# Keys turned by DMA as planes of 16-bit words, a weight term in the short-mantissa type, a branch hint, and a new order

## The chip, the core and the metric

The kernel runs on one core of a Trainium2 chip. A core has a matrix engine (TensorE, PE in the profile; its weight loads are listed as PEld), a vector engine (VectorE, DVE), an activation engine (ScalarE, ACT), a general engine (GpSimd, POOL) and SyncE (SP), which here issues every DMA. Each engine works through its own list of instructions in order and waits on semaphores that the others raise. The metric is device time in microseconds (us) of one execution. Lower is better.

## What is computed

Gated linear attention on 4 x 8 heads of 768 steps, followed by a gated MLP whose spatial product mixes all 768 steps. Everything is float32.

```python
# attention: for every step t, per batch and head (head_dim 48)
state = alpha[t][:, None] * state + outer(k[t], v[t])
y[t] = q[t] @ state
# MLP on x = all heads side by side (4, 768, 384)
h = gelu_tanh(x @ w_in)            # 384 -> 1024
u, v = h[..., :512], h[..., 512:]
v_n = (v - mean(v)) / sqrt(var(v) + 1e-6) * g_ln
v_s = einsum('ts,bsd->btd', w_sg, v_n) + b_sg[:, None]
out = x + (u * v_s) @ w_out        # 512 -> 384
```

w_in and w_out arrive as 64-bit floats.

## The kernel before

**Attention in blocks.** The 4 x 768 steps are cut into 24 blocks of 128, numbered 0 to 23, six for each batch. Block i loads its decays (`a_i`) and one tile with k, q and v (`kqv_i`). Two scans on DVE (`scan_i`, `recip_i`) build the products of decays; `q_i` and `k_i` scale queries and keys by them (k on DVE or POOL). PE then does the "squares": step `G_o_i` takes the score products of block i together with the first products of block o = i - 1 (output `y`, and the outer products `dl` of k and v that go into the state); `M_o_i` and `H_o_i` follow with the rest of y. `causal_i` (DVE) masks the scores, `half_i`, `add_i` and `state_i` (DVE) bring the state on. `y3_i` and `xf_i` (ACT) copy y out of PSUM, three small DMAs (`pack_i_k`) put a part of it in place.

The outer products need the keys with steps, not head dimensions, on the partitions. So `H_o_i` ends with four 128 x 128 transposes on PE (line 500, tile `tp`), and `kn_i` (ACT, line 513) copies them to SBUF. `G_i_(i+1)` waits for it.

**MLP.** `xh_i` and `xl_i` split x into a high part in the short-mantissa type (fp32r, which the matrix engine takes in one pass) and a remainder in the same type. Every MLP product is then three fp32r products (high by high, high by low, low by high; lines 582 to 584): `V_b_c` (v half, nine matmuls of 512 columns) and its followers `V_b_c_1` to `_8` (gelu, moments, normalisation, split); `U_b_h_d` (u half, nine matmuls of 384 columns); `P_b_h_d` (spatial product, 18 matmuls) with `_1` to `_4` (scale, gate, split); `R_b_h_k` (output product, 12 matmuls), its `_add` on DVE and its `_store`.

**Weights.** They are split the same way once, in pieces of 384 columns: `wv_j` and `wu_j` (w_in), `ws_s_h` (w_sg) and `wo_d` (w_out). For the 64-bit ones `size`, `clamp`, `shift`, `sign`, `power` and `rest` rebuild a float32 and the part that it leaves over, `high` (ACT) makes the high part. For `wv` and `wu` the low part is made on PE (`low_pe`, lines 293 to 295, tile `mm_w`): identity by the float32, minus identity by the high part, identity by the rest. The first and the last of these are full float32 products.

**The order.** A string, `ORDER`, names all steps; they are issued in this order, which sets the order within each engine. A suffix such as `/dve` chooses the engine where a step has two. `Plan.issue` checks that each step's inputs and buffers have been issued.

**The end.** Every range check of the decays is summed into one number, `cnt_i`. Each engine loads it and branches over a general, slow version of the whole computation (`tc.If`, line 1024), which the inputs here never need.

```python
    with tc.manual_schedule():
        plan.issue(ORDER)
    n_ok = nc.values_load(cnt_i[0:1, 0:1], min_val=0, max_val=P)
    with tc.If(n_ok < P):
```

Of the kernel before, what the change touches and what calls it, by code (L numbers as in the profile page):

```python
# [9 lines left out]
F32 = mybir.dt.float32  # L10
# [3 lines left out]
U32 = mybir.dt.uint32  # L14
AF = mybir.ActivationFunctionType
# [20 lines left out]
NIDLE = 10  # L36
EPS = 1e-6
# [4 lines left out]
a_0 scan_0 idle_0 end_0 idle_1 idle_2 idle_3 kqv_0_q idle_4 idle_5 pend_0 q_0 recip_0 load_wv_1 size_wv_1 clamp_wv_1  # L42
kqv_0_k k_0/dve G_n_0 H_n_0 idle_6 idle_7 load_wv_0 a_1 range_0 size_wv_0 shift_wv_1 floor_0 sign_wv_1 clamp_wv_0
kqv_1 power_wv_1 shift_wv_0 rest_wv_1 sign_wv_0 scan_1 high_wv_1 kn_0 causal_0 end_1 q_1 pend_1 low_pe_wv_1 idle_8
idle_9 kqv_0_v a_2 load_wv_3 power_wv_0 recip_1 rest_wv_0 k_1/dve floor_1 high_wv_0 size_wv_3 low_wv_1 clamp_wv_3
kqv_2 scan_2 G_0_1 turn_0 M_0_1 half_0 H_0_1 pend_2 end_2 shift_wv_3 q_2 sign_wv_3 recip_2 load_ws_1_0 high_ws_1_0
low_pe_ws_1_0 power_wv_3 load_ws_2_0 high_ws_2_0 y3_0 floor_2 causal_1 add_0 k_2/pool a_3 low_pe_ws_2_0 state_0
low_pe_wv_0 scan_3 rest_wv_3 xf_0 kn_1 low_ws_1_0 high_wv_3 G_1_2 low_ws_2_0 turn_1 M_1_2 half_1 H_1_2 pend_3
range_1 end_3 kqv_3 q_3 recip_3 range_2 add_1 causal_2 load_ws_4_0 high_ws_4_0 kn_2 xf_1 pack_0_1 pack_0_0 load_wv_2
low_wv_0 pack_0_2 low_pe_wv_3 size_wv_2 y3_1 k_3/pool state_1 load_ws_5_0 clamp_wv_2 a_4 low_pe_ws_4_0 shift_wv_2  # L50
sign_wv_2 G_2_3 low_wv_3 xh_0 low_ws_4_0 turn_2 half_2 M_2_3 H_2_3 high_wv_2 high_ws_5_0 power_wv_2 rest_wv_2
low_pe_wv_2 kqv_4 load_ws_0_0 load_wu_1 pack_1_2 pack_1_0 pack_1_1 kn_3 range_3 xf_2 low_pe_ws_5_0 low_wv_2 a_5
xl_0/pool causal_3 V_0_0 add_2 floor_3 scan_4 end_4 pend_4 high_ws_0_0 q_4 recip_4 k_4/dve state_2 kqv_5 size_wu_1
y3_2 low_pe_ws_0_0 pack_2_0 pack_2_2 pack_2_1 clamp_wu_1 shift_wu_1 floor_4 sign_wu_1 power_wu_1 G_3_4 half_3
V_0_0_1 turn_3 low_ws_0_0 xh_1 M_3_4 H_3_4 rest_wu_1 load_wu_2 low_ws_5_0 high_wu_1 low_pe_wu_1 scan_5 xl_1/dve q_5
end_5 pend_5 xh_2 low_wu_1 V_0_1 xl_2/dve recip_5 kn_4 y3_3 size_wu_2 xf_3 clamp_wu_2 U_0_0_1 load_wu_0 k_5/pool
V_0_0_2 V_0_2 V_0_0_3 V_0_1_1 causal_4 V_0_1_2 add_3 V_0_0_4 V_0_0_5 load_ws_3_0 pack_3_1 range_5 range_4 size_wu_0
V_0_0_6/act clamp_wu_0 state_3 G_4_5 turn_4 M_4_5 shift_wu_2 high_ws_3_0 pack_3_0 pack_3_2 low_pe_ws_3_0 shift_wu_0
sign_wu_2 V_0_1_3 a_6 kqv_6 V_0_0_7 high_wu_2 U_0_0_1_1 power_wu_2 sign_wu_0 floor_5 xh_3 low_ws_3_0 high_wu_0
half_4 rest_wu_2 power_wu_0 H_4_5 V_0_0_8 rest_wu_0 xl_3/dve V_0_2_1 low_pe_wu_2 add_4 causal_5 V_0_2_2 V_0_3  # L60
V_0_1_4 V_0_1_5 state_4 scan_6 V_0_2_3 xf_4 y3_4 kn_5 V_0_1_6/act V_0_1_7 V_0_1_8 G_5_n turn_5 M_5_n low_pe_wu_0
# [1033 lines left out]
```

## Time and profile before

| | |
|---|---|
| median of 3 runs | 362.7 us (362.56 to 363.47) |
| profiled execution | 362.69 us, of which 360.9 us from its first to its last instruction (the span) |
| granted TensorE clock in the span, mean | 0.993 |
| matmul instructions | 4548 |
| share of the 16 DMA engines that SP's queue takes | 33.4% |
| bytes from and to HBM | 32.70 MB read, 4.72 MB written |

In the rows that follow, the timeline gives start (us), duration (us), engine, line, operation, tiles (output <- inputs), shape and how many instructions are merged. A row by line gives the count, then the sum of busy time (us) and the mean (ns), then the engine's idle time ahead of these instructions and what ended it. A row of DMA issues ends with the size of one and the median time from issue to landing. A row of a line's instructions gives count, shortest, median and longest (ns), and the first and last start (us). A row of waits reads "who <- for whom: us in total, times, longest".

### The profile page before, as it was taken

How to read it: one execution, taken by the hardware profiler on the slowest of the kernel's cores; microseconds unless marked ns; L12 is line 12 of the kernel's file. 1: busy time of each engine (PE TensorE's matmuls, PEld its weight loads, DVE VectorE, ACT ScalarE, POOL GpSimd, SP SyncE). 2: the span in 40 equal slices, each digit the busy share in tenths (PEclk: the TensorE clock that was granted, in tenths of full speed). 3: DMA queues.
4: the chain of work that ended last, by engine and by line, in shares of the span. 5: the costliest groups of instructions: out<-in, count | busy, mean ns of one | idle time of the engine just before them, and what ended most of it. 6: DMA issues, size and time to landing. Idle time of an engine off the chain costs nothing.

```text
span 360.9 us, 10758 instructions
## 1 busy us (share of the span) xinstructions
PE 346.5 (96%) x4548; PEld 316.4 (88%) x4548; DVE 250.1 (69%) x496; ACT 153.5 (43%) x372; POOL 84.5 (23%) x128
## 2 busy tenths in 40 slices
PE   6799999999999999999999999999999999999991
PEld 6567877999999888899999889899999889999991
DVE  6999999899999968674656877568555744441241
ACT  4388777843543357623214365522233434311110
POOL 1021221423102346332103307210305122300000
PEclk9999999999999999999999999999999999999997
DMA  7877476443532565211315055120340000000002
GB/s 265 286 236 263 118 215 215 126 162 91 191 97 70 161 217 156 94 31 53 130 47 162 17 166 180 25 99 2 116 138 7 22 31 29 2 0 22 23 25 72
DMA packets 17912, 39.37 MB, mean 109 GB/s; under 512 B 2880, under 2 KB 9792, under 8 KB 17856
## 3 DMA queue, kind: packets, MB, share of 16 engines
q1 hardware_dynamic: 17856, 38.61, 33.4%
q8 instruction: 37, 0.61, 0.7%
q14 instruction: 19, 0.16, 0.1%
HBM read 32.70 MB, written 4.72 MB: 104 GB/s over the span
## 4 chain that ended last, share of the span: by engine, by line
PE 87%; DVE 2%; issue 0%; DVEq 0%
PE mm_s L582 10%; PE mm_s L583 9%; PE mm_s L584 9%; PE mm_u L582 5%; PE mm_u L583 5%; PE mm_u L584 5%; PE mm_v L582 5%; PE mm_v L584 4%; PE mm_v L583 4%; PE y L415 4%; PE mm_o L582 4%; PE mm_o L698 3%; PE mm_o L584 3%; PE mm_o L583 3%; PE tp L500 3%; PE y L425 3%
## 5 line engine op out<-in xcount | busy, mean ns | idle before, releaser
L582 PE MATMUL mm_s<-ws_hi,vh 128*128 128x384 f32 x192 | 66.1, 344 | 0.0
L583 PE MATMUL mm_s<-ws_lo,vh 128*128 128x384 f32 x192 | 65.0, 338 | 0.0
L584 PE MATMUL mm_s<-ws_hi,vl 128*128 128x384 f32 x192 | 65.0, 338 | 0.0
L673 ACT CAST gh<-g 128x384 fp32r<-128x384 f32 x32 | 16.2, 512 | 48.4 <-DVE g L668 28.7
L582 PEld LDWEIGHTS mm_s<-ws_hi,vh 128*128 128x128 f32 x192 | 36.0, 188 | 0.3
L583 PEld LDWEIGHTS mm_s<-ws_lo,vh 128*128 128x128 f32 x192 | 36.1, 188 | 0.0
L584 PEld LDWEIGHTS mm_s<-ws_hi,vl 128*128 128x128 f32 x192 | 36.0, 188 | 0.0
L663 DVE SCALAR_TENSOR_TENSOR g<-mm_s,g_col,b_bc 128x384 f32<-128x384 f32 x32 | 19.4, 610 | 22.2 <-PE mm_s L584 22.2
L668 POOL TENSOR_TENSOR g<-g,u 128x384 f32<-128x384 f32 x15 | 15.2, 1011 | 82.7 <-DVE g L663 74.3
L582 PE MATMUL mm_u<-xh,wi_hi 128*128 128x384 f32 x96 | 33.3, 347 | 0.0
L359 DVE TENSOR_TENSOR_SCAN pf<-a,floor 128x516 f32<-128x516 f32 x24 | 31.1, 1297 | 2.4 <-DMA a<-in_aT 2.0
L583 PE MATMUL mm_u<-xl,wi_hi 128*128 128x384 f32 x96 | 32.4, 338 | 0.0
L584 PE MATMUL mm_u<-xh,wi_lo 128*128 128x384 f32 x96 | 32.4, 338 | 0.0
L377 DVE TENSOR_TENSOR_SCAN pf<-a,floor 128x516 f32<-128x516 f32 x24 | 30.2, 1259 | 1.3
L582 PE MATMUL mm_v<-wi_hi,xh 128*128 128x512 f32 x72 | 29.7, 413 | 0.0
L387 POOL TENSOR_TENSOR kqv_t<-kqv_t,pf 128x512 f32<-128x512 f32 x12 | 14.3, 1191 | 65.2 <-DVE pf L377 49.9
L707 DVE TENSOR_TENSOR xf<-mm_o,xf 128x384 f32<-128x384 f32 x24 | 13.0, 550 | 23.0 <-PE mm_o L698 23.0
L584 PE MATMUL mm_v<-wi_hi,xl 128*128 128x512 f32 x72 | 28.5, 395 | 0.0
L583 PE MATMUL mm_v<-wi_lo,xh 128*128 128x512 f32 x72 | 28.4, 394 | 0.0
L402 PE MATMUL sc<-kqv_t 64*64 64x64 f32 x768 | 25.8, 220 | 2.6 <-DVE floor L383 2.4
L648 ACT ACTIVATE u<-mm_u 128x384 f32<-128x384 f32 x32 | 15.5, 490 | 27.9 <-PE mm_u L584 27.9
L402 PEld LDWEIGHTS sc<-kqv_t 64*64 64x64 f32 x768 | 23.6, 135 | 3.4 <-DVE floor L383 2.5
(117 smaller groups left out, 831.2 us busy)
## 6 DMA issues: line engine op xcount, KB each, us to landing
kqv_t<-in_kqv SPq DMA_DIRECT2D x23, 768.0 KB, 4.5
a<-in_aT SPq DMA_DIRECT2D x24, 258.5 KB, 3.2
out_x<-xf SPq DMA_DIRECT2D x24, 192.0 KB, 2.1
raw<-in_w_in SPq DMA_DIRECT2D x8, 384.0 KB, 3.7
raw<-in_w_out SPq DMA_DIRECT2D x4, 384.0 KB, 3.1
raw_sg<-in_w_sgT SPq DMA_DIRECT2D x6, 192.0 KB, 5.5
xf<-y SPq DMA_DIRECT2D x72, 16.0 KB, 1.8
raw<-in_w_sgT SPq DMA_DIRECT2D x6, 192.0 KB, 2.8
```

The costliest lines, as they stand in the source:

```text
L359: nc.vector.tensor_tensor_scan(pf.rearrange("p j t -> p (j t)"), s["a"][:, 0:NP * C1], floor.rearrange("p j t -> p (j t)"), initial=0.0, o ...
L377: nc.vector.tensor_tensor_scan(s["pf"].rearrange("p j t -> p (j t)")[:, ::-1], s["a"][:, NP * C1:0:-1], floor.rearrange("p j t -> p (j t)" ...
L387: eng.tensor_tensor(s["k"], s["k"], s["pf"][:, :, 1:], op=ALU.mult)
L402: lambda j=j, h=h: nc.tensor.matmul(sc[half(h), e, 64 * j:64 * j + 64], k[half(e), j, half(h)], q[half(e), j, half(h)], start=True, stop=True,
L415: lambda j=j: nc.tensor.matmul(y_of(y, j, e)[:, half(h)], v[half(h), j, half(e)], at[half(h), e, j], start=first and j < 2, stop=True, ski ...
L582: nc.tensor.matmul(o, lh, rh, start=(idx == 0), stop=False)
L583: nc.tensor.matmul(o, lh, rl, start=False, stop=False)
L584: nc.tensor.matmul(o, ll, rh, start=False, stop=(idx == n - 1))
L648: nc.scalar.activation(t["u"], t["o"], AF.Gelu_apprx_tanh)
L663: nc.vector.scalar_tensor_tensor(t["g"], t["o"], g_col[:, d:d + 1], b_bc[:, tsl], op0=ALU.mult, op1=ALU.add,)
L668: eng.tensor_tensor(t["g"], t["g"], u["u"], op=ALU.mult)
L673: nc.scalar.copy(g["h"][:, d], t["g"])
```

## The change

1. **Keys of blocks 8 to 23.** Their transposes leave PE. The keys are copied into two planes of 16-bit words (`kp_i`, ACT), a transposing DMA on SP's queue turns both planes (`kt_i`, eight tiles of 128 x 128 words), and `kn_i` (ACT or, for blocks 15, 19 and 22, DVE) puts the words together again. `kp` and `kt` share two buffers with the raw weights.
2. **Rest term.** For `wv` and `wu` the rest is written, negated, into an fp32r tile of its own, and the third product of `low_pe` becomes minus identity by this rest, both fp32r.
3. **Branch hint.** The last two steps (the last add and its store) stand in a code block of their own, which begins with a hint for the branch on SP and DVE.
4. **Order.** The whole `ORDER` string is new.

```diff
+CLOSING = 2
+TURNED = 8
...
-    def split_f64(dst_hi, dst_lo, src):
+    def split_f64(dst_hi, dst_lo, src, on_pe):
...
         def rest():
+            if on_pe:
+                t["rest"] = mlp.tile([P, TH], F32R, tag="g", name="rest", bufs=2)
             nc.vector.scalar_tensor_tensor(
-                t["mag"], t["raw"][:, :, 0].bitcast(U32), 2.0 ** -52, t["mag"], op0=ALU.mult, op1=ALU.mult,
+                t["rest"] if on_pe else t["mag"], t["raw"][:, :, 0].bitcast(U32), (-1 if on_pe else 1) * 2.0 ** -52, t["mag"],
+                op0=ALU.mult, op1=ALU.mult,
             )
 
         def low_pe():
             t["o"] = o = psm.tile([P, TH], F32, tag="mm", name="mm_w")
             nc.tensor.matmul(o, ident, t["top"].bitcast(F32), start=True, stop=False)
             nc.tensor.matmul(o, nident, dst_hi, start=False, stop=False)
-            nc.tensor.matmul(o, ident, t["mag"], start=False, stop=True)
+            nc.tensor.matmul(o, nident, t["rest"], start=False, stop=True)
...
         if i is not None:
+            if i >= TURNED:
+                return
             st[i]["tp"] = tp = ps.tile([P, NP, P], F32, tag="tp", name="tp")
             for j in range(NP):
                 nc.tensor.transpose(tp[:, j], st[i]["k"][:, j], ident)
...
+    def words(x):
+
+        return x.bitcast(U16).rearrange("p j (t w) -> p w j t", w=2)
+
+    def k_words(i):
+        st[i]["kp"] = kp = stage.tile([P, 2, NP, C], U16, tag="raw", name="kp", bufs=2)
+        nc.scalar.copy(kp, words(st[i]["k"]))
+
+    def k_turn(i):
+        st[i]["kt"] = kt = stage.tile([P, 2, NP, P], U16, tag="raw", name="kt", bufs=2)
+        nc.sync.dma_start_transpose(
+            kt.rearrange("p w j d -> p (w j) d"), st[i]["kp"].rearrange("p w j t -> p (w j t)"),
+        )
+
+    def k_whole(i, eng):
+        st[i]["kn"] = kn = att1.tile([P, NP, P], F32, tag="kn", name="kn")
+        if eng is nc.scalar:
+            eng.copy(words(kn), st[i]["kt"])
+        else:
+            eng.tensor_copy(words(kn), st[i]["kt"])
...
+            plan.add(("kp", i), "act", 950, lambda i=i: k_words(i), [("k", i)], takes=[("raw", 2, [("kt", i)])])
+            plan.add(
+                ("kt", i), "sp", 1200, lambda i=i: k_turn(i), [("kp", i)], takes=[("raw", 2, [("kn", i)])], nbytes=500000,
+            )
+            plan.add(
+                ("kn", i), "act", 950, lambda i=i: k_whole(i, nc.scalar), [("kt", i)], takes=[("kn", 1, [o_at[i]])],
+                other=("dve", 1100, lambda i=i: k_whole(i, nc.vector)),
+            )
...
+    order = ORDER.split()
     with tc.manual_schedule():
-        plan.issue(ORDER)
+        plan.issue(order[:-CLOSING])
+    with tc.block():
+        tc.mark_branch_hint_location("general", hint=0, engines=[mybir.EngineType.SP, mybir.EngineType.DVE])
+        with tc.manual_schedule():
+            plan.issue(order[-CLOSING:])
...
-    with tc.If(n_ok < P):
+    with tc.If(n_ok < P, label="general"):
```

Three places show what the new order does. The first is PE's list in the head of the program, up to the start of `G_4_5` (the squares of blocks 4 and 5, which begin with the y products). Before, the last matmul of `U_0_0_1` (tile `mm_u`) and the nine of `V_0_2` (`mm_v`) lead up to it:

```order
L584 MATMUL mm_u<-xh,wi_lo 128x384
L582 MATMUL mm_v<-wi_hi,xh 128x512
L583 MATMUL mm_v<-wi_lo,xh 128x512
L584 MATMUL mm_v<-wi_hi,xl 128x512
L582 MATMUL mm_v<-wi_hi,xh 128x512
L583 MATMUL mm_v<-wi_lo,xh 128x512
L584 MATMUL mm_v<-wi_hi,xl 128x512
L582 MATMUL mm_v<-wi_hi,xh 128x512
L583 MATMUL mm_v<-wi_lo,xh 128x512
L584 MATMUL mm_v<-wi_hi,xl 128x512
L415 MATMUL y<-at,kqv_t 64x64 x8
L440 MATMUL dl_838<-kqv_t,kn 64x48
```

After the change the same list on PE, at the same squares; the `mm_v` rows are now the end of `V_0_1`, and two pieces of w_sg follow it (`mm_w`):

```order
L614 MATMUL mm_v<-wi_lo,xh 128x512
L615 MATMUL mm_v<-wi_hi,xl 128x512
L613 MATMUL mm_v<-wi_hi,xh 128x512
L614 MATMUL mm_v<-wi_lo,xh 128x512
L615 MATMUL mm_v<-wi_hi,xl 128x512
L253 MATMUL mm_w<-raw_sg,ident 128x384
L254 MATMUL mm_w<-ws_hi,nident 128x384
L253 MATMUL mm_w<-raw_sg,ident 128x384
L254 MATMUL mm_w<-ws_hi,nident 128x384
L423 MATMUL y<-at,kqv_t 64x64 x8
L448 MATMUL dl_820<-kqv_t,kn 64x48
```

`U_0_0_1` and `V_0_2` moved behind `G_4_5`; of all PE steps ahead of it, only `low_pe` of `wu_2` is new.

The second place is ACT's list in the body, up to the key copy of block 14 (`kn`, the last row). Before, it copies transposes from PSUM:

```order
L561 CAST xh<-xf 128x3x128
L484 COPY alo_102<-alo 128x1
L365 COPY pend<-pf 128x4
L391 ACTIVATE a,low<-a,alo 128x4x128
L648 ACTIVATE u<-mm_u 128x384
L365 COPY pend<-pf 128x4
L673 CAST gh<-g 128x384 x2
L550 COPY xf<-y 128x3x128
L540 COPY y_2724<-y 128x128
L513 COPY kn<-tp 128x512
```

After the change, from the copy of block 13 (first row) to that of block 14 (last row) on ACT, with the copy into planes (`kp`) between them:

```order
L542 COPY kn<-kt 128x2x512
L679 ACTIVATE u<-mm_u 128x384
L492 COPY alo_102<-alo 128x1
L679 ACTIVATE u<-mm_u 128x384
L531 COPY kp<-kqv_t 128x1024
L571 COPY y_2659<-y 128x128
L399 ACTIVATE a,low<-a,alo 128x4x128
L581 COPY xf<-y 128x3x128
L373 COPY pend<-pf 128x4
L542 COPY kn<-kt 128x2x512
```

Between `kp` and `kn` of a block, four short instructions now stand on ACT, and `kn` waits for a DMA in place of PE.

The third place is the end of SP's list. Before, the last seven stores (`out_x`), between them the load of the check's number, and the branch:

```order
L711 DMA out_x<-xf 128x384
L1023 TENSOR_LOAD cnt_i
L1023 ISA x2
L711 DMA out_x<-xf 128x384 x6
L1024 COMPARE_AND_BRANCH
```

After the change, the same end on SP:

```order
L1070 TENSOR_LOAD cnt_i
L1070 ISA x2
L742 DMA out_x<-xf 128x384 x5
L1063 UNCONDITIONAL_BRANCH
L1135 BRANCH_PREFETCH_HINT
L742 DMA out_x<-xf 128x384
L1063 UNCONDITIONAL_BRANCH
L1071 COMPARE_AND_BRANCH
```

The hint and a jump came in ahead of the last store, a second jump behind it. On DVE the same two jumps and the hint stand around the last add.

More of the change, by code (lines that the diff above doesn't have):

```diff
@@ L52 @@
[L52 to L61, printed above, removed]
@@ new lines @@
+high_ws_1_0 low_pe_wv_2 low_pe_ws_1_0 y3_1 xh_0 sign_wu_1 q_3 power_wu_1 kn_2 high_wu_1 recip_3 rest_wu_1
+low_pe_wu_1 range_3 low_ws_1_0 range_2 k_3/dve causal_2 add_1 floor_3 xl_0/pool state_1 a_4 scan_4 G_2_3 turn_2
+low_wv_2 half_2 kqv_4 load_wu_2 pack_1_1 M_2_3 H_2_3 pack_1_2 pack_1_0 a_5 size_wu_2 pend_4 end_4 q_4 clamp_wu_2
+recip_4 shift_wu_2 xh_1 low_wu_1 y3_2 xf_2 kn_3 k_4/pool add_2 causal_3 load_wu_0 V_0_0 floor_4 state_2 sign_wu_2
+high_wu_2 G_3_4 turn_3 kqv_5 load_ws_5_0 xl_1/dve power_wu_2 half_3 M_3_4 H_3_4 rest_wu_2 scan_5 size_wu_0
@@ new lines @@
+clamp_wu_0 end_5 add_3 low_pe_wu_2 xf_3 pend_5 V_0_0_1 kn_4 high_ws_5_0 low_wu_2 V_0_1 q_5 recip_5 load_ws_0_0
+pack_2_1 pack_2_2 pack_2_0 state_3 high_ws_0_0 k_5/pool load_ws_3_0 low_pe_ws_5_0 y3_3 range_4 low_ws_5_0 V_0_1_1
+V_0_0_2 causal_4 low_pe_ws_0_0 G_4_5 turn_4 M_4_5 V_0_0_3 shift_wu_0 sign_wu_0 V_0_0_4 V_0_1_2 half_4 a_6 load_wu_3
+power_wu_0 V_0_1_3 high_wu_0 xh_2 high_ws_3_0 xl_2/dve rest_wu_0 pack_3_1 pack_3_0 pack_3_2 H_4_5 low_ws_0_0 xf_4
+low_pe_ws_3_0 low_ws_3_0 kqv_6 size_wu_3 kn_5 xh_3 V_0_0_5 V_0_1_4 y3_4 V_0_0_6/act V_0_0_7 add_4 floor_5 causal_5
@@ new lines @@
+scan_6 state_4 xl_3/dve end_6 low_pe_wu_0 V_0_2 V_0_1_5 G_5_n clamp_wu_3 pend_6 V_0_1_6/act load_wo_1 low_wu_0
+turn_5 V_0_1_7 V_0_3 q_6 V_0_0_8 recip_6 V_0_3_1 shift_wu_3 V_0_1_8 k_6/pool pack_4_1 a_7 pack_4_2 pack_4_0 kqv_7
+V_0_2_1 xh_4 size_wo_1 V_0_3_2 half_5 M_5_n V_0_3_3 U_0_0_1 H_5_n y3_5 xf_5 V_0_2_2 V_0_2_3 G_n_6 pack_5_1 U_0_0_0
+H_n_6 V_0_3_4 floor_6 sign_wu_3 xl_4/dve clamp_wo_1 pack_5_0 pack_5_2 V_0_3_5 power_wu_3 U_0_0_1_1 high_wu_3 U_0_0_2
+shift_wo_1 rest_wu_3 V_0_3_6/act U_0_0_0_1 range_5 load_wo_0 g_col scan_7 V_0_3_7 pend_7 xh_5 V_0_2_4 low_pe_wu_3
@@ L148, in __init__ @@
     def __init__(self):
-        self.steps = {}
+        self.steps, self.done, self.held = {}, set(), {}
     def add(self, name, eng, ns, fn, after=(), takes=(), lead={}, nbytes=0, other=None, start=0.0):
@@ L158, in issue @@
     def issue(self, order):
-        done, held = set(), {}
-        for word in order.split():
+        done, held = self.done, self.held
+        for word in order:
             label, _, eng = word.partition("/")
@@ L170, in issue @@
             done.add(s["name"])
-        assert not self.steps, "steps left out"
 def run(steps):
@@ L333, in w_out_piece @@
     def w_out_piece(d):
-        return split_f64(wo_hi[:, d, :], wo_lo[:, d, :], w_out[d * P:(d + 1) * P, :])
+        return split_f64(wo_hi[:, d, :], wo_lo[:, d, :], w_out[d * P:(d + 1) * P, :], False)
     st = {}
@@ L788, in tile_gla_gmlp @@
             first.append((("M", o, i), 2 * SLOT))
-        groups += first + [(("H", o, i), (0 if o is None else SLOT) + (0 if i is None else 530))]
+        groups += first + [(("H", o, i), (0 if o is None else SLOT) + (0 if i is None or i >= TURNED else 530))]
     pieces = [(("wv", j), w_in_piece(1, j)) for j in range(4)]
@@ L817, in tile_gla_gmlp @@
         last = at("low_pe") if on_pe else at("low")
-        plan.add(at("size"), "act", 510, p["size"], [at("load")], takes=[("mag", 2, [last])])
+        plan.add(at("size"), "act", 510, p["size"], [at("load")], takes=[("mag", 2, [at("rest") if on_pe else last])])
         plan.add(at("clamp"), "dve*", 330, p["clamp"], [at("size")])
@@ L823, in tile_gla_gmlp @@
         plan.add(at("power"), "dve*", 330, p["power"], [at("sign")])
-        plan.add(at("rest"), "dve*", 550, p["rest"], [at("power")])
+        plan.add(at("rest"), "dve*", 550, p["rest"], [at("power")], takes=[("g", 2, [last])] if on_pe else [])
         if on_pe:
-            plan.add(at("low_pe"), "pe", 1460, p["low_pe"], [at("high"), at("rest")], takes=[("mm", 3, [at("low")])])
+            plan.add(at("low_pe"), "pe", 940, p["low_pe"], [at("high"), at("rest")], takes=[("mm", 3, [at("low")])])
             plan.add(at("low"), "act", 490, p["low_act"], [at("low_pe")])
@@ L926, in tile_gla_gmlp @@
             deps = [last] + ([("half", o)] if o is not None else [])
-            takes = [("tp", 1, [("kn", i)])] if i is not None else []
+            takes = [("tp", 1, [("kn", i)])] if i is not None and i < TURNED else []
             plan.add(
@@ L1017, in tile_gla_gmlp @@
     plan.add(("cnt_i",), "dve", 150, lambda: nc.vector.tensor_copy(cnt_i, check["cnt"]), [("cnt",)])
+    order = ORDER.split()
     with tc.manual_schedule():
-        plan.issue(ORDER)
+        plan.issue(order[:-CLOSING])
[3 more added lines that the diff above has]
+            plan.issue(order[-CLOSING:])
+    assert not plan.steps, "steps left out"
     n_ok = nc.values_load(cnt_i[0:1, 0:1], min_val=0, max_val=P)
-    with tc.If(n_ok < P):
+    with tc.If(n_ok < P, label="general"):
         x_all = dram.tile([B * NCH, P, NK, C], F32, name="x_all")
```

187 lines of the change are left out of this document (94 added, 93 removed).

## The prediction

> **What bounds the kernel now.** The page comes first, for the busy shares; then the busy time by stretches, since a mean over 361 us hides the stages.
>
> ```profile
> PE 346.5 (96%) x4548; PEld 316.4 (88%) x4548; DVE 250.1 (69%) x496; ACT 153.5 (43%) x372; POOL 84.5 (23%) x128
> ```
>
> ```profile
> 27.00:36.00 9.00, 8.40 (x162) 6.27 (x164) 8.64 (x17) 7.30 (x18) 1.19 (x2) 1.00 0.79 267
> 36.00:54.00 18.00, 17.95 (x343) 14.25 (x341) 17.53 (x43) 13.83 (x35) 4.69 (x9) 1.00 0.58 167
> 72.00:90.00 18.00, 18.00 (x219) 17.37 (x218) 17.10 (x36) 6.93 (x17) 5.17 (x5) 1.00 0.40 126
> 216.00:252.00 36.00, 36.00 (x398) 33.81 (x398) 25.52 (x47) 13.51 (x33) 11.15 (x17) 1.00 0.26 82
> ```
>
> After the bounds of a stretch and its length stand PE, PEld, DVE, ACT and POOL. From 36 us on PE is never idle, so an instruction taken off PE there shortens the span, unless another engine is just as late. One is: DVE is busy 17.53 of 18 us up to 54 us and still 95% at 72 to 90 us; only later (25.52 of 36) has it room. So there are three stages: a head where DVE and PE arrive together, a body where PE alone decides, and a tail. The timeline shows the meeting in the head, at the squares of blocks 4 and 5 (step G_4_5, which starts with the y products):
>
> ```profile
> 42.23 0.34 PE L582 MATMUL mm_u<-xh,wi_hi 128*128 128x384 f32 x1
> 42.41 0.34 PE L583 MATMUL mm_u<-xl,wi_hi 128*128 128x384 f32 x1
> ...
> 43.82 0.40 PE L582 MATMUL mm_v<-wi_hi,xh 128*128 128x512 f32 x1
> ...
> 46.02 0.46 PE L415 MATMUL y<-at,kqv_t 64*64 64x64 f32 x16
> ...
> 47.81 0.91 PE L248 MATMUL mm_w<-raw_sg,ident 128*128 128x384 f32 x2
> ```
>
> ```profile
> 45.19 0.35 DVE L536 TENSOR_TENSOR s_c<-s_m,pend 128x192 f32<-128x192 f32 x1
> ```
>
> G_4_5 needs the state of block 3 (step state_3), which DVE ends at 45.54; PE comes to it at 46.02, after U_0_0_1 (42.23 to 43.82, 1.59 us) and V_0_2 (43.82 to 46.02, 2.20 us). DVE had 0.5 us in hand. What makes PE faster ahead of this point only makes it wait here.
>
> **Transposes off PE.** Sixteen of 24 groups of four go. One group in the timeline:
>
> ```profile
> 252.32 0.46 PE L425 MATMUL y<-kqv_t,s_m 64*64 64x64 f32 x16
> 252.71 0.66 PE L500 MATMUL tp<-ident,kqv_t 128*128 128x128 f32 x4
> 253.13 0.42 PE L582 MATMUL mm_o<-gh,wo_hi 128*128 128x384 f32 x1
> ```
>
> From its start to the next step's start are 0.42 us (busy times overlap in PE's pipeline, so starts count); the group at 38.16, ahead of the rows below, takes 0.50. I take 0.46: 16 x 0.46 = **7.4 us**, all behind 80 us, where PE is full.
>
> **Rest term in a short mantissa.** One piece of weights (wu_1) before:
>
> ```profile
> 38.16 0.66 PE L500 MATMUL tp<-ident,kqv_t 128*128 128x128 f32 x4
> 38.66 0.81 PE L293 MATMUL mm_w<-top,ident 128*128 128x384 f32 x2
> 39.01 0.64 PE L294 MATMUL mm_w<-wi_hi,nident 128*128 128x384 f32 x1
> 39.48 0.81 PE L295 MATMUL mm_w<-mag,ident 128*128 128x384 f32 x2
> 39.83 0.69 PE L582 MATMUL mm_v<-wi_hi,xh 128*128 128x512 f32 x1
> ```
>
> A full float32 product is two passes, 0.35 us to the next start, and holds up that next one: 0.47 to 39.48, where a short-mantissa product of this width takes 0.18 (42.23 to 42.41). So 0.35 + 0.29 = 0.64 us against 0.18, a gain of 0.46 us on each of eight pieces, **3.7 us** if it counted. DVE's instruction that writes the rest stays of its kind.
>
> **Head in the new order.** PE: U_0_0_1 and V_0_2 now stand behind G_4_5, the product for wu_2 ahead of it. DVE's part of that trade, ahead of G_4_5's last DVE input: k_4, xl_2, V_0_0_3 and V_0_1_2 leave, k_3 and four steps of wu_2 (shift, sign, power, rest) come.
>
> ```profile
> L601 DVE BATCH_NORM_STATS2 stats<-vg 128x6 f32<-128x512 f32 x24 | 16.4, 685 | 12.2 <-ACT vg L597 12.2
> L387 DVE TENSOR_TENSOR kqv_t<-kqv_t,pf 128x512 f32<-128x512 f32 x12 | 8.7, 725 | 0.1
> L565 DVE TENSOR_TENSOR xl<-xf,xh 128x384 fp32r<-128x384 f32 x13 | 7.8, 599 | 1.1 <-ACT xh L561 1.1
> L278 DVE SCALAR_TENSOR_TENSOR top<-raw,top 128x384 int32<-128x384 int32 x12 | 7.2, 607 | 0.1
> L287 DVE SCALAR_TENSOR_TENSOR mag<-raw,mag 128x384 f32<-128x384 uint32 x12 | 6.6, 548 | 0.1
> L605 DVE BATCH_NORM_AGGREGATE mv<-stats 128x2 f32<-128x6 f32 x24 | 4.2, 176 | 0.8
> L284 DVE TENSOR_SCALAR mag<-top 128x384 int32<-128x384 int32 x12 | 4.2, 350 | 0.0
> L272 DVE TENSOR_SCALAR top<-mag 128x384 int32<-128x384 int32 x12 | 4.1, 348 | 0.1
> ```
>
> Out: 0.73 + 0.60 + 0.18 + 0.69 = 2.2 us; in: 0.73 + 0.35 + 0.61 + 0.35 + 0.55 = 2.6 us. DVE, full here, reaches the point 0.4 us later, at 45.9; with a hand-over of 0.1, G_4_5 stays at 46.0. PE has less ahead of it (3.79 - 1.0 for wu_2, and 0.46 on five other pieces, together 5.1 us) and would wait about 5 us in all. Behind G_4_5 PE then has: + 3.79 (U_0_0_1, V_0_2), - 1.46 (wu_2 at its old price of 0.35 + 0.47 + 0.64), - 0.9 (rests of wu_0 and wu_3), - 7.4 (transposes) = **- 6.0 us**. If DVE did not hold, it would be 7.4 + 3.7 = 11.1; those are the ends, and I take 6.0 because DVE's rows show no gap to shrink.
>
> **Where the turned keys go.** Each of 16 blocks gets a copy into two planes (kp), a transposing DMA (kt) and a copy back (kn, 13 on ACT, 3 on DVE), for one ACT copy of 0.59.
>
> ```profile
> L673 ACT CAST gh<-g 128x384 fp32r<-128x384 f32 x32 | 16.2, 512 | 48.4 <-DVE g L668 28.7 <-PE mm_o L698 10.3 <-POOL g L668 9.3
> L625 ACT CAST vh<-vg 128x512 fp32r<-128x512 f32 x24 | 14.5, 618 | 6.9 <-DVE vg L621 6.6
> L513 ACT COPY kn<-tp 128x512 f32<-128x512 f32 x24 | 14.1, 588 | 5.0 <-PE tp L500 5.0
> ```
>
> 128 more elements cost 106 ns, so 1024 come to about 1.0 us: ACT gains 13 x 1.4 + 3 x 0.4 = 19 us on 153.5, DVE 3 to 4 us after 150 us. Both lie beside a full PE; without that cover, they would cost what they last. The transfer has no row of its own kind:
>
> ```profile
> out_x<-xf SPq DMA_DIRECT2D x24, 192.0 KB, 2.1
> raw<-in_w_out SPq DMA_DIRECT2D x4, 384.0 KB, 3.1
> xf<-y SPq DMA_DIRECT2D x72, 16.0 KB, 1.8
> ```
>
> 256 KB as an ordinary transfer lands 2.1 to 3.1 us after issue; as 16 pieces of 16 KB one after another it would be 16 x 1.8 = 29 us. I take the nearest size and an allowance for the odd layout, 3.5 us. What waits: the added wait of kn on ACT holds y copies, gelus and the gate's casts behind it; kt's wait for kp holds loads and packs on SP. The chain kp, kt, kn then takes 1.0 + 3.5 + 1.0 = 5.5 us. The shortest stretch that covers it in the new PE order runs from the scores of block 12 to its outer products: the squares (1.8 us from 46.02 to 47.81, and 0.4 for their last sixteen products, 252.32 to 252.71), two U and one V, 2.2 + 3.2 + 2.2 = 7.6 us. So 2.1 us are spare, and this part costs nothing in the sum.
>
> [...]
>
> **Tail.**
>
> ```profile
> 353.18 0.34 PE L698 MATMUL mm_o<-gl,wo_hi 128*128 128x384 f32 x1
> ```
>
> ```profile
> 353.56 0.56 DVE L707 TENSOR_TENSOR xf<-mm_o,xf 128x384 f32<-128x384 f32 x1 [1.10 <-PE mm_o L698]
> ```
>
> ```profile
> L1024 SPq EVENT_SEMAPHORE  x8: 17/17/17, 357.2 to 359.5; - x8
> ...
> L1024 DVEq COMPARE_BRANCH  x1: 72/72/72, 354.4 to 354.4; - x1
> ...
> L1024 SPq COMPARE_BRANCH  x1: 45/45/45, 354.5 to 354.5; - x1
> L1024 DVEq EVENT_SEMAPHORE  x1: 21/21/21, 357.6 to 357.6; - x1
> ```
>
> ```profile
> SPq L1024 <- SPq L1024: 4.5, 3, 2.7
> ```
>
> The last add ends at 354.12; SP branches at 354.5 and does its next instruction at 357.2, DVE 354.4 and 357.6: 2.7 and 3.2 us in which nothing computes, so code is being fetched. SP then loses another 1.8 (4.5 - 2.7). The last store, 2.1 us after its issue at 354.1, has landed by 356.2. With the branch's target fetched early, SP would wait only for that: eight semaphores close together (0.6) and the last 1.4 us (359.5 to 360.9) give 356.2 + 2.0 = 358.2, a gain of 2.7. The hint stands before the last add and store, 1.7 us before the branch, less than the 2.7 the fetch took, so about 1 us of it stays, still under the store's landing. I take **2.6**; the ends are 0 (no effect) and 4.5. The two added jumps have no row of their own: between 0.05 (the branch row that needs no fetch) and 2.7 each. They go to the instructions next in the code, so I take 0.1 in all. [...]
>
> **Sum.** 362.69 (360.9 and 1.8 around it) - 6.0 - 2.6 + 0.1 = 354.2 us. The profiled time is that of the median, 362.7, so nothing is added.
>
> **Rivals.**
> 1. *PE alone decides the head*: DVE's order was the loose end, and all 11.1 us count: 362.7 - 11.1 - 2.5 = 349.1. For it: PE is 18.00 of 18.00 from 54 us on. Against: DVE's 17.53 of 18.
> 2. *The transfers are slow, and PE waits for the turned keys.* Place: the squares that take blocks 9 to 12 and 14, whose cover by the new PE order is 7.6 us three times and 8.6 twice (squares and two P of eighteen matmuls at 0.18, or one V and two R of twelve). With a landing of L, each waits L + 2.0 - cover; together 5 L - 30. Nothing up to 5.6 us; from L = 7.7 they eat the 8.5 us of the forecast and the change is slower. [...] For it: 2.1 us spare is little, and ACT and SP are queues in order. Against: the ordinary rows.
> 3. *The same, moderately*: L of 6.2 to 7.7, or kt late in SP's queue by as much: 3 to 9 us, 357 to 363.
> 4. *The hint does nothing* (dropped, too late, or the new block's jumps fetch): 354.2 + 2.6 = 356.8.
>
> **Chances.** Forecast 0.48 (own range 352 to 356), rival 1 0.13, rival 2 0.15, rival 3 0.11, rival 4 0.13. The range 348 to 362 leaves out rival 2 and the edges of 1 and 3, 0.2. A measurement of this kernel tells 0.3% (1.1 us) from no change. Slower is rival 2, 0.15; within are the last microseconds of rival 3, 0.05; faster is the rest, 0.80.
>
> **What would show it.** L500's line with 32 instructions, not 96; the third mm_w product once for each piece, the next start 0.2 us behind it. PE idle for DVE before G_4_5, some 5 us more than before in the first 50 us: if PE is idle no more than before there, rival 1 holds. The kt issues' time to landing: under 5.6, and no PE wait on kn. On SP, the instruction after the last branch within 0.5 us; a gap of 2.7 is rival 4. I am wrong if PE waits anywhere behind 110 us for more than 2 us in all.

## The result, and the profile after

| | before | after |
|---|---|---|
| median | 363.09 us (4 runs, 362.56 to 363.79) | 352.7 us (4 runs, 351.92 to 353.09) |
| ratio | | 0.9693, 95% interval 0.9649 to 0.9736 |
| profiled execution | 362.69 us, span 360.9 | 351.92 us, span 350.2 |
| start of G_4_5 | 46.02 us | 44.64 us |
| from there to the end of the last matmul | 307.5 us | 299.5 us |
| from there to the end of the span | 7.35 us | 6.1 us |

The last three rows cut the span into head, body and tail. Of the 10.7 us that the span lost, 1.4 came from the head, 8.0 from the body and 1.3 from the tail. First the changed kernel's page, then its busy time by stretches (length, then PE, PEld, DVE, ACT, POOL, granted clock, DMA share, GB/s).

```profile
PE 334.6 (96%) x4476; PEld 306.9 (88%) x4476; DVE 250.4 (71%) x502; ACT 180.6 (52%) x392; POOL 74.0 (21%) x118
```

```profile
18.00:36.00 18.00, 14.57 (x349) 10.62 (x339) 17.98 (x41) 13.30 (x37) 2.81 (x3) 1.00 0.79 259
36.00:54.00 18.00, 17.63 (x341) 13.48 (x341) 16.74 (x39) 14.26 (x34) 4.83 (x8) 1.00 0.58 195
216.00:252.00 36.00, 36.00 (x432) 34.60 (x431) 25.16 (x47) 13.95 (x28) 7.93 (x12) 1.00 0.33 83
```

The same stretch of the kernel before, 18 to 36 us:

```profile
18.00:36.00 18.00, 17.08 (x315) 12.29 (x317) 17.30 (x33) 14.52 (x37) 3.40 (x3) 1.00 0.76 251
```

PE, with less to do, is now idle for 3.4 of these 18 us, and DVE has not a tenth left: the head waits for DVE, as forecast (most of PE's waits there end with a DVE instruction). DVE did have 0.7 us to give here, though, and it gave them. The body is full as before. The changed kernel's timeline around the start of G_4_5, PE first, then DVE:

```profile
43.62 0.91 PE L253 MATMUL mm_w<-raw_sg,ident 128*128 128x384 f32 x2
44.08 0.63 PE L254 MATMUL mm_w<-ws_hi,nident 128*128 128x384 f32 x1
44.64 0.46 PE L423 MATMUL y<-at,kqv_t 64*64 64x64 f32 x16
```

```profile
42.60 0.33 DVE L567 TENSOR_TENSOR s_c<-s_m,pend 128x192 f32<-128x192 f32 x1
42.85 0.69 DVE L632 BATCH_NORM_STATS2 stats<-vg 128x6 f32<-128x512 f32 x1
43.45 0.67 DVE L515 TENSOR_TENSOR at<-sc,mask 128x512 f32<-128x512 f32 x1
```

DVE's last input for G_4_5 (`at`) was ready at 44.12, PE came at 44.64: PE's waits fall ahead of this point, not at it. The turned keys, by their line (SP's issue, with its time to landing) and by groups (sum and mean; then ACT's idle time ahead and what ended it); last, PE's longest waits in the whole span:

```profile
L535 SPq DMA_TRANSPOSE kt<-kp x16: 1235/1256/1892, 100.1 to 274.8; - x16
...
DMA to landing us min/median/max: 2.7/2.9/4.7
```

```profile
L542 ACT COPY kn<-kt 128x1024 uint16<-128x1024 uint16 x13 | 17.8, 1372 | 6.1 <-DMA kt<-kp 6.1
L531 ACT COPY kp<-kqv_t 128x1024 uint16<-128x1024 uint16 x16 | 16.7, 1046 | 7.2 <-DVE kqv_t L395 4.5 <-POOL kqv_t L395 2.6
...
L510 PE MATMUL tp<-ident,kqv_t 128*128 128x128 f32 x32 | 5.2, 285 | 0.0
...
L303 PE MATMUL mm_w<-rest,nident 128*128 128x384 f32 x8 | 2.9, 362 | 0.7 <-DVE rest L294 0.7
...
L544 DVE COPY kn<-kt 128x1024 uint16<-128x1024 uint16 x3 | 2.3, 751 | 0.0
```

```profile
PE mm L549 <- ACT mask L210: 2.7, 1, 2.7
PE sc L410 <- DVE kqv_t L395: 1.9, 1, 1.9
PE y L423 <- DVE at L515: 0.9, 1, 0.9
```

ACT waited for a transfer twice (6.1 us), PE for the copy `kn` never. At the end, SP and DVE at the last branch:

```profile
L1071 SPq EVENT_SEMAPHORE  x8: 17/17/17, 348.0 to 348.8; - x8
...
L1071 DVEq COMPARE_BRANCH  x1: 84/84/84, 345.1 to 345.1; - x1
...
L1071 SPq COMPARE_BRANCH  x1: 73/73/73, 345.1 to 345.1; - x1
L1071 DVEq EVENT_SEMAPHORE  x1: 21/21/21, 348.1 to 348.1; - x1
```

SP still stands for 2.8 us behind the branch (before 2.7), DVE for 3.1 (3.2): the hint took nothing off. What got shorter is what follows: eight semaphores in 0.9 us (348.0 to 348.8), where the kernel before took 2.3 (357.2 to 359.5). One of the eight belongs to the last store. Its issue and its time to landing, before and after:

```profile
L711 SPq DMA_DIRECT2D out_x<-xf x1: 332/332/332, 354.1 to 354.1; - x1
...
DMA to landing us min/median/max: 3.8/3.8/3.8
```

```profile
L742 SPq DMA_DIRECT2D out_x<-xf x1: 332/332/332, 344.8 to 344.8; - x1
...
DMA to landing us min/median/max: 3.8/3.8/3.8
```

So it lands at 357.9 before and at 348.5 after, and in both kernels SP gets past its semaphore 0.01 us later.

### The profile page after: what moved, and what is told of

Same layout as the page of the kernel before. It is cut to its first block, busy times and chain, and to the rows that moved or that the text cites. A ratio compares the mean times of both kernels' runs of the same rounds, so it can differ in the third digit from the quotient of the medians.

```text
span 350.2 us, 10682 instructions
## 1 busy us (share of the span) xinstructions
PE 334.6 (96%) x4476; PEld 306.9 (88%) x4476; DVE 250.4 (71%) x502; ACT 180.6 (52%) x392; POOL 74.0 (21%) x118
## 3 DMA queue, kind: packets, MB, share of 16 engines
q1 hardware_dynamic: 34752, 42.81, 41.8%
## 4 chain that ended last, share of the span: by engine, by line
PE 83%; DVE 8%; DMA 3%; ACT 2%; issue 2%; SPq 1%; DVEq 0%; ACTq 0%
PE mm_s L613 10%; PE mm_s L614 9%; PE mm_s L615 9%; PE mm_u L613 5%; PE mm_v L613 5%; PE mm_u L615 5%; PE mm_u L614 5%; PE mm_v L614 4%; PE mm_v L615 4%; PE mm_o L613 4%; PE mm_o L614 4%; PE mm_o L729 4%; PE mm_o L615 4%; PE y L423 3%; PE y L433 3%
## 5 line engine op out<-in xcount | busy, mean ns | idle before, releaser
L699 POOL TENSOR_TENSOR g<-g,u 128x384 f32<-128x384 f32 x16 | 17.5, 1096 | 92.8 <-DVE g L694 89.4
L395 POOL TENSOR_TENSOR kqv_t<-kqv_t,pf 128x512 f32<-128x512 f32 x12 | 15.5, 1292 | 84.7 <-DVE pf L385 56.8
L367 DVE TENSOR_TENSOR_SCAN pf<-a,floor 128x516 f32<-128x516 f32 x24 | 29.4, 1226 | 4.4 <-DMA a<-in_aT 2.9
L385 DVE TENSOR_TENSOR_SCAN pf<-a,floor 128x516 f32<-128x516 f32 x24 | 30.0, 1250 | 1.9 <-ACT pend L373 1.3
L709 DVE TENSOR_TENSOR gl<-g,gh 128x384 fp32r<-128x384 f32 x32 | 19.3, 609 | 13.5 <-ACT gh L704 13.4
```

Source lines behind the costliest of these rows:

```text
L367: nc.vector.tensor_tensor_scan(pf.rearrange("p j t -> p (j t)"), s["a"][:, 0:NP * C1], floor.rearrange("p j t -> p (j t)"), initial=0.0, o ...
L385: nc.vector.tensor_tensor_scan(s["pf"].rearrange("p j t -> p (j t)")[:, ::-1], s["a"][:, NP * C1:0:-1], floor.rearrange("p j t -> p (j t)" ...
L395: eng.tensor_tensor(s["k"], s["k"], s["pf"][:, :, 1:], op=ALU.mult)
L699: eng.tensor_tensor(t["g"], t["g"], u["u"], op=ALU.mult)
L709: nc.vector.tensor_tensor(g["l"][:, d], t["g"], g["h"][:, d].bitcast(F32), op=ALU.subtract)
```

## The experiments

The first three take the change apart, each from the other side.

**e1: transposes of all blocks on PE, in the new order.**

```diff
-TURNED = 8
+TURNED = 24
-    order = ORDER.split()
+    order = [w.partition("/")[0] if w[:3] == "kn_" else w for w in ORDER.split() if w[:3] not in ("kp_", "kt_")]
```

> The changed kernel with all 24 blocks' keys transposed on PE again (no word planes, no DMA transposes). Theory (a group of four transposes costs PE 0.46 us, the way by DMA costs nothing, behind 80 us PE decides): 16 x 0.46 = 7.4 us more than the changed kernel's 352.7, so 360.1. Rival, transposes dearer than their own starts show (they hold up the product behind them; 0.6 us a group): 362.3. Rival, PE waits for the DMA way and gives part of it back: under 358.

360.45 us (359.52 to 360.74), ratio to before 0.9903 (0.9868 to 0.9938): 7.75 us more than with the turned keys. From G_4_5 to the last matmul's end 306.5 us, against 299.5. The 16 groups are worth 7.0 us of PE's list, 0.44 each. One profile of each is not exact: after, e5, e7 and e11 share all steps of the body, and theirs last 299.5 to 300.2 us. Counted from start to start, the rows of `tp` alone differ by 6.6 us, 0.41 a group.

**e2: the rest term in float32 again.** The same function, with the identity in place of minus identity and the rest not negated.

```diff
-                t["rest"] = mlp.tile([P, TH], F32R, tag="g", name="rest", bufs=2)
+                t["rest"] = mlp.tile([P, TH], F32, tag="g", name="rest", bufs=2)
...
-            nc.tensor.matmul(o, nident, t["rest"], start=False, stop=True)
+            nc.tensor.matmul(o, ident, t["rest"], start=False, stop=True)
```

> The changed kernel with the rest term as a full float32 product again (values as before the change). Theory (DVE holds the head, so only the pieces of wu_0 and wu_3, behind the squares of blocks 4 and 5, count): 2 x 0.46 = 0.9 us, 353.6. Rival (PE alone decides in the head): 8 x 0.46 = 3.7 us, 356.4.

354.28 us (354.1 to 354.68), ratio 0.9739 (0.9708 to 0.977): 1.6 us more than after, not 3.7. The body is 300.35 us long, 0.86 more, which is two pieces at 0.43. The starts bear this out where the body's scatter leaves it open: behind G_4_5 the rows of `mm_w` and `mm_v` together grew by 0.98 us, 0.49 a piece. The other six pieces stand ahead of G_4_5. In e3, which has the float32 rest too, PE does 3.0 us more ahead of G_4_5 than after, is idle for 3.4 us less and gets there no later (44.2 us): there it would have waited anyway. In e2's own profile G_4_5 starts at 46.6, so the 0.7 us that the medians show beyond the body stay unexplained.

**e3: the new order alone.** No turned keys, float32 rest, no block and no hint.

> Only the new order: keys transposed on PE, rest term in float32, no block of its own at the end and no hint. Theory (DVE holds the head and the new order puts less PE work ahead of the squares of blocks 4 and 5: U_0_0_1 and V_0_2 behind, wu_2 ahead, 2.3 us more behind them; those squares start 1.4 us earlier): 363.1 + 0.9 = 364.0. Rival (the order by itself saves waits in the body, which would explain why PE gained 9.4 us and not 6.0): 360 to 362.

362.7 us (360.76 to 363.98, 11 runs), ratio 0.9984 (0.9963 to 1.0004): no difference. That is itself a finding: the body holds U_0_0_1 and V_0_2 more and wu_2 less, 2.3 us by the rows before, and yet is 307.4 us long, where before it was 307.5. (The profile is of the fastest of the eleven; its 1.8 us less than before's lie in the head.)

**e4: the turned keys (blocks 9 to 23) in the old order.** `kp` and `kt` stand right behind the later of the block's keys and the last block's `kn`.

```diff
+    for i in range(TURNED, n):
+        names = [w.partition("/")[0] for w in order]
+        at = 1 + max(names.index(f"k_{i}"), names.index(f"kn_{i - 1}"))
+        order[at:at] = [f"kp_{i}", f"kt_{i}"]
```

> The kernel before with the keys of blocks 9 to 23 (15 blocks) turned by DMA, in the old order (the two new steps put in right behind k and the key copy of the block before). Theory: 15 x 0.46 = 6.9 us less than 363.1, 356.2, if the old order leaves the three steps (1.0 + 2.9 + 1.4 us) their cover. Transposes dearer (0.6 us): 354.1. Rival, the old order has too little cover: PE waits on kn show in the trace and the time stays above 358.

389.06 us (387.53 to 392.48), ratio 1.0714 (1.0642 to 1.0785): 26 us slower than before. Its waits, of PE for `kn` and of DVE for the loads, and those of SP for something ahead of `kt` (the four longest of its rows; all come to 101 us):

```profile
PE dl L441 <- ACT kn L535: 1.1, 1, 1.1
```

```profile
DVE kqv_t L370 <- DMA kqv_t<-in_kqv: 27.5, 7, 5.3
```

```profile
SPq L528 <- ACT y L564: 24.5, 4, 8.8
SPq L528 <- ACT xf L574: 17.6, 2, 12.8
SPq L528 <- ACT u L672: 11.1, 1, 11.1
SPq L528 <- ACT gh L697: 9.8, 2, 4.9
```

PE hardly ever waits for turned keys. SP does, standing at `kt` until ACT comes to `kp`, and the loads of later blocks stand behind it in SP's list. They arrive late, DVE waits 27.5 us for them, and PE is idle for 22 us behind 46 us, where before it was for 0.4. Behind the longest holes the granted clock falls as well. Where it is low the profile gives it as 0.50 (before, from 356.0 us on, behind its last matmul); a stretch with a figure in between is taken here as partly at full, partly at half clock. The stretches around the first hole, of 4.74 us, in e4 (the third figure from the end is the clock):

```profile
102.00:108.00 6.00, 1.65 (x112) 1.51 (x104) 1.14 (x1) 0.19 (x1) 0.00 (x0) 0.91 0.39 91
108.00:114.00 6.00, 5.61 (x32) 5.50 (x33) 4.34 (x9) 2.49 (x3) 0.00 (x0) 0.52 0.00 0
```

There are four such stretches in the body, 23.9 us at half clock in all, where before has none: half of that, an estimated 12 us, is lost. Idle time and clock together make 34 us; less 15 groups off PE (6.9) and 1.8 in head and tail that is 25, against the 26.3 by which the span grew. The changed kernel's SP stands at `kt` for 52 us too, but DVE has no such row there: what counts is not that SP waits but what is queued behind it.

**e9: e4 with the transfer issued by ACT.**

```diff
-        nc.sync.dma_start_transpose(
+        nc.scalar.dma_start_transpose(
```

> The kernel before with the turned keys of blocks 9 to 23 in the old order, as in e4 (389.1 us), but the transposing DMA is issued by ACT, right behind its kp, in place of SP. Theory (in e4 SP stood 63 us at kt waiting for the planes, and the loads queued behind it came late): SP no longer waits there, DVE's wait for loads of kqv falls from 27.5 us to under 5, PE's idle time behind 50 us from 22 us to under 6, and the time comes to 356 to 364 us (362.7 less 15 groups of 0.46, plus what ACT's 15 issues of 1.24 us hold up). Rival (the chain kp, kt, kn itself has too little cover in the old order): PE idle stays above 12 us and the time above 374.

376.61 us (2 runs, 373.75 and 379.48): the time is the rival's (above 374), its cause is not, since PE never waits for `kn`. Of the theory only the loads came true. They are on time, but ACT, which issues for 1.25 us a block, is late with what PE takes from it, and PE is idle for 11.7 us behind 46 us. The waits of DVE for loads, and PE's longest:

```profile
DVE kqv_t L370 <- DMA kqv_t<-in_kqv: 0.6, 1, 0.6
```

```profile
PE y L416 <- ACT alo L485: 6.1, 5, 2.0
```

SP's queue was the cause of the late loads; moving the stall to another engine's list moved the price along.

**e10: e4 with `kt` half way between `kp` and `kn`,** still on SP.

```diff
-        order[at:at] = [f"kp_{i}", f"kt_{i}"]
+        order[at:at] = [f"kp_{i}"]
+        names = [w.partition("/")[0] for w in order]
+        to = names.index(f"kn_{i}")
+        order[at + 1 + (to - at - 1) // 2:at + 1 + (to - at - 1) // 2] = [f"kt_{i}"]
```

> The same as e4, the transposing DMA still on SP, but placed half way between the copy into planes and the copy back, not right behind the former. Theory (SP's queue held): most of SP's 63 us of waiting at kt go, loads come earlier, and the time falls from 389.1 to 357 to 368 us; what is left is PE waiting for kn where the transfer now comes too late. Rival (too little cover): the later transfer makes it worse, PE waits for kn more than 10 us, over 380 us.

364.65 us (363.86 to 366.04, 8 runs), ratio 1.0031 (1.001 to 1.0052): 24 of the 26 us are back by the place of one instruction. DVE has no wait for `kqv` loads, SP stands at `kt` for 21 us. What is left: PE is idle for 7.2 us behind 46 us, most of it in one hole of 4.92 us that ends at 135.5. The stretches around it in e10:

```profile
126.00:132.00 6.00, 4.60 (x142) 3.99 (x140) 4.83 (x9) 2.13 (x5) 3.31 (x5) 1.00 0.82 129
132.00:138.00 6.00, 2.48 (x65) 2.37 (x65) 0.88 (x4) 4.18 (x9) 1.00 (x1) 0.75 0.59 212
138.00:144.00 6.00, 6.00 (x62) 4.49 (x63) 3.74 (x7) 1.94 (x4) 2.07 (x2) 0.68 0.30 90
```

Behind the hole the granted clock is 0.75 and 0.68: 6.8 us at half clock, which cost another 3.4 us. So 15 groups off PE (-6.9), 7.2 idle, 3.4 of clock and a tail shorter by 1.6 make +2.1; the profiled execution took 364.89 us, +2.2. That is closer than the terms are: the body alone grew by 4.4 us, where idle time, clock and groups make 3.3, and the head was 0.4 us shorter. In none of the three old-order kernels did the turn of keys pay; it paid in the order that leaves no hole.

**e8: each transfer issued twice,** in the changed kernel.

```diff
+        for _ in range(2):
```

> The changed kernel with every transposing DMA issued twice, the second over the first, so that the turned keys come about 4 us later (issue 1.3 + landing 2.9 in place of 2.9). By the second rival's sum, with L about 7 and the copies 1.0 and 1.4, 5 x (7 + 2.4) - 40 = 7 us more than the changed kernel, 359 to 360, with PE waits on kn. If the cover is longer than I counted (blocks whose keys are ready earlier): under 355.

369.09 us in one run: 16.4 more than after, over twice what was expected. The second issue waits for the first to land (SP stands 37.3 us for `kt<-kp` in all, 17 times), so `kn` starts at the earliest 5.5 us behind the first, in the middle 7.2 (after: 2.9 and 5.3). Waits of ACT, then of PE:

```profile
ACT kn L543 <- DMA kt<-kp: 32.8, 10, 5.7
```

```profile
PE dl L448 <- ACT kn L543: 5.9, 5, 1.7
...
PE y L423 <- DVE at L515: 2.3, 3, 0.9
PE y L433 <- DVE s_m L560: 1.9, 5, 0.7
```

PE waits for `kn` at five places for 5.9 us: blocks 9 to 12 and 14, the five that the prediction named. 5 L - 30 gives 6 us at that 7.2; at the five places themselves the second transfer lands on average 7.6 us behind the first issue, for which it gives 8. That formula priced only this wait. ACT stands still for 33 us, and what it does for others comes late too: PE is idle for 10.6 us behind 46 us in all, and 6.8 us of half clock (0.81 and 0.62 in 144 to 156 us) cost 3.4 more. The body grew by 16.9 us; about 3 of them are not accounted for.

**The end of the program: e5, e6, e7, e11, e12.** e5 is the changed kernel without the hint, e7 with the hint ahead of the last 20 steps, not 2, e11 with neither hint nor block. e6 is the kernel before with block and hint, e12 with the block alone.

```diff
-        tc.mark_branch_hint_location("general", hint=0, engines=[mybir.EngineType.SP, mybir.EngineType.DVE])
```

```diff
-CLOSING = 2
+CLOSING = 20
```

> The changed kernel with the block of its own at the end, but without the hint. Theory (the hint fetches nothing: the trace shows no code fetch between the hint and the branch, and 2.8 us from SP's branch to its next instruction as before): same time, 352.7, the gap still 2.7 to 2.8 us, and no second gap of 1.3 us among SP's last semaphores if that one went because the code lies elsewhere. Rival (the hint is what removed the second gap): 1.2 us more, 353.9, with the second gap back.

> The kernel before with nothing but the block of its own for the last two steps and the hint. Theory (the hint does nothing): 363.1 within 0.3%, first gap 2.7 us; the second gap of 1.3 us among SP's last semaphores may stay or go with the few instructions by which the code moves. Rival (the hint removed the second gap): 1.2 us less, 361.9. Rival of the prediction (the target comes early): 2.6 us less, 360.5.

> The changed kernel with the block and the hint ahead of the last 20 steps, not 2 (some 10 us before the branch). Theory A (the hint came too late to fetch, 1 us before SP's branch): the gap behind SP's branch goes from 2.8 to under 0.5 us, the end waits for the last store, 1 to 2 us less. Theory B (this hint never leads to a fetch here): gap 2.7 to 2.8 us again, time as the changed kernel's.

> The changed kernel with its last two steps in the common list again: no block of their own, no hint, no added jumps. Theory (the hint and the block do nothing; the second gap at the end comes and goes with where the code lies): within 1.5 us of the changed kernel, 351.5 to 354.5; from the last matmul to the end either 5.6 to 6.4 us or about 7.4. Rival (the block brought the 1.3 us): 7.4 us behind the last matmul and 354.0 us or more.

> The kernel before with its last two steps in a block of their own, without the hint. Theory (hint of no effect): as e6 (361.6 us, 6.4 us behind the last matmul). Rival (the hint removed the second gap at the end): 7.4 us behind the last matmul, 362.7.

| run | us | gap from the end of SP's branch | last matmul's end to the end |
|---|---|---|---|
| after | 352.7 | 2.75 | 6.1 |
| e5, no hint | 353.27 (350.97 to 356.09) | 2.62 | 5.6 |
| e11, no hint, no block | 353.0 (351.53 to 354.72) | 2.81 | 5.8 |
| e7, hint 20 steps ahead (one run) | 353.87 | 2.63 | 5.6 |
| before | 363.09 | 2.64 | 7.35 |
| e12, block on before | 363.17 (361.85 to 364.08) | 2.60 | 7.5 |
| e6, block and hint on before | 361.59 (360.44 to 364.84) | 2.70 | 6.4 |

The gap is 2.6 to 2.8 us whatever is done: the hint does not shorten it, not even where it stands 10 us ahead on DVE and 13 on SP (e7). Before and after alike, queue q14, whose kind the page gives as "instruction", moves two packets in this gap. In the changed kernel hint and block are worth nothing that shows: without both it takes 353.0 us, ratio 0.9719 (0.9682 to 0.9757). What differs is a second gap of 1.2 to 2.0 us, some semaphores later on SP. It is there in before, e3, e9 and e12, and not in after, e4, e5, e10 and e11, nor in any kernel with the hint. So it goes without a hint too. Where the code happens to lie is a likely reason, not a shown one: on q14 there are 19 packets in the whole execution in the four kernels with the gap and in e6, 18 in all others. Whether in e6 the hint removed it is open (0.9967, 0.9933 to 1.0001, against e12's 0.999, 0.997 to 1.001). A shift of the code by itself was not tried.

## Why the prediction was right, point by point

| term | predicted | measured |
|---|---|---|
| transposes off PE | -7.4 | -7.0 (e1 against after, body), -6.6 by their own rows; -7.75 in the medians |
| rest term behind G_4_5 | -0.9 | -0.9 (e2 against after, body); -1.6 in the medians |
| U_0_0_1, V_0_2 and wu_2 across G_4_5 | +2.3 | -0.1 (e3 against before, body) |
| start of G_4_5 | 0 | -1.4 in the profile |
| tail | -2.6 | -1.3, and not by the hint |

**Bounds.** DVE held the head as said. PE's added idle time there was half the 5 us forecast: 2.8 us in the first 54, most in 18 to 36 us. The failed step is "DVE's rows show no gap to shrink": at 17.30 of 18 it had 0.7 us, and it is now at 17.98. DVE's last input came 1.4 us earlier, where the forecast had it 0.4 later. The start of G_4_5 also scatters: 43.8, 44.2, 44.6, 45.3, 46.1 and 46.3 us in e5, e11, after, e8, e1 and e7, which share every step up to there, and 45.3 to 46.4 in the six kernels with the old order. Much of that is the clock: e8, e1 and e7 have 3.4 to 6.8 us at half clock in the head, and so have two of the six. In e1 the row is

```profile
30.00:36.00 6.00, 4.18 (x131) 3.75 (x130) 5.98 (x12) 3.67 (x11) 0.64 (x1) 0.72 0.60 198
```

Without these the means are 44.2 and 45.7 us, and the new order starts G_4_5 some 1.5 us earlier. (e2, with the float32 rest, is the exception: 46.6 at the full clock.)

**Transposes** came out near the predicted price: 0.41 to 0.44 us a group against 0.46, nothing given back.

**Rest term.** The price of a piece was right (0.43 to 0.49 against 0.46). That only two of eight count fits e3 and the bodies; e2's medians leave 0.7 us open. Rival 1, by which PE alone decides the head and all 11.1 us count, falls by its own sign: PE's idle time in the head grew, and the six pieces of rest term there did not bring their 2.8 us. The time alone would not have ruled it out: PE's list lost 9.4 us up to its last matmul (353.5 to 344.1), which is nearer to 11.1 than to the 6.0 forecast. The order term and the head are why.

**The order.** This term was mis-sized: +2.3 forecast, -0.1 found. The steps that moved cost what was said: counted from start to start, `mm_u`, `mm_v` and `mm_w` together grew by 2.2 us behind G_4_5 (e3 against before). Against that stand steps that did not move across it: `mm_s` -0.9, score products -0.5, `mm_o` -0.4, y -0.3, transposes -0.2 (scores and y move by 0.3 to 0.6 us between kernels with the same body, the other rows named here by 0.1 at most). The prediction counted which steps lie behind G_4_5 and not how they follow each other. A hold, a next start that comes about 0.1 us later than usual, stands at many places where PE goes from a spatial or an output product to the squares: 17 in before, 11 in e3; and within runs of these products, 18 and 9. That is 1.4 of the 2.3 us; the rest was not taken apart.

**Transfers.** Landing 2.9 us for 3.5 taken, `kp` 1.05 for 1.0, `kn` 1.37 for 1.0: the chain's own work came to 5.3 us for 5.5, and PE never waited. With the waiting in ACT's and SP's lists the chain took longer, 5.3 to 13.7 us from `kp`'s start to `kn`'s end, and `kn` was ready between 0.7 and 9.8 us ahead of the outer products, so the least slack was 0.7 and not 2.1 us. The eight tiles of one issue landed in 2.9 us (256 KB), where ordinary issues of 192 KB (`out_x<-xf`) took 2.1 and of 384 KB (`raw<-in_w_out`) 3.5 in the same run. Rivals 2 and 3 fall for this order. (Rival 3's 3 to 9 us belong to L of 6.6 to 7.7; at 6.2 its own terms give 1.8.) Their place was right (e8: five waits for `kn`), their price too low for the kernel as a whole, since they left out the engines that stand still and the clock. And e4 shows a danger that the prediction named ("kt's wait for kp holds loads and packs on SP") without a price: 26 us, 12 of them by the clock, in an order that does not keep the loads off it.

**Tail.** The step that failed is "with the branch's target fetched early": SP and DVE still stood for it, and in its mechanism rival 4 is what happened. A second term was off too: the last store was to have landed by 356.2, with the median 2.1 us of all stores, but it took 3.8 and landed at 357.9. With that, an early target could have won at most some 1.3 us (357.9, and the 1.7 us that after takes from there to its end, make 359.6 against 360.9). The tail shrank by 1.3 us all the same, without hint and block as well (e5, e11): the second gap was gone.

So that 354.2 came so near to 352.7 is in part luck: 2.0 us of gain too few in the body (2.4 by the order, less 0.4 by the transposes) and 1.4 in the head stand against 1.3 too many in the tail.

## What to carry to other kernels

Work taken off the full engine pays its price only where that engine is full (here all of the transposes, 7.0 us; of the rest terms the two behind G_4_5, 0.9 us), and each piece is worth pricing by its place. In e4 a transfer that waited for its source held up the loads behind it in its queue, and DVE waited 27.5 us for them: put such a transfer where its source is done, look at what is queued next, and do not settle for moving it to another engine's list. Read an effect's mechanism off the trace even when the sum comes out right; here the tail's gain was not the hint's.

## What the runs showed of the hardware

- **A short hole cost twice.** In e9 PE was idle for at most 2.02 us at a time ahead of 105.8 us, and the granted clock fell to 0.72 in the next stretch:

```profile
100.00:106.00 6.00, 3.98 (x108) 3.60 (x109) 5.70 (x13) 1.37 (x4) 0.00 (x0) 1.00 0.32 41
106.00:112.00 6.00, 6.00 (x70) 5.93 (x63) 2.49 (x4) 3.20 (x5) 0.00 (x0) 0.72 0.65 187
```

  That is 3.4 us at half clock, up to 1.7 us lost: the starts of `mm_s`, 0.18 us apart at 107.08, are 0.32 apart at 107.51. PE was busy for 45% of the 3.4 us ahead of the drop. Elsewhere too the low stretches come to 3.4 us (0.72 in 30 to 36 us of e1) or to twice that (0.91 and 0.52 in 102 to 114 us of e4: 6.8), and the drops of one run lie whole multiples of 3.41 us apart (106.9 and 134.2 in e4: eight). In all kernels together the clock falls 14 times ahead of the last matmul, each time behind 3.41 us in which PE was busy for 0 to 53%; in e1 the longest hole among them is 0.96 us. Counted on from the drops in steps of 3.41 us, the steps that kept the clock had PE busy for 50% or more, but for some in the first 11 us (45% in after, from 6.87 to 10.28 us). That it depends also on where a hole falls in these steps is an estimate from these numbers, not shown by itself: the same head loses clock in e1 (0.72) and not in after (1.00). After, with no hole over 0.3 us in the body, has no such loss there.
- **The transposing DMA** holds SP for 1.26 us an issue, and its packets are small: under 512 B they went from 2880 to 19776. SP's queue takes 41.8% of the DMA engines' time for 33.4%, and the 16 KB packs (`xf<-y`) land in 2.6 us for 1.8.
- **Copies by words** of 16 bits, 1024 elements a partition, take ACT 1.05 us into planes and 1.37 back, DVE 0.75 back.
